# Moving the first transposes of a batch behind the GEMM before them, on one core of a fused attention and feed-forward kernel

## The chip, the cores and the metric

The kernel runs on one core of a Trainium2 chip. The metric is the device time of one execution in microseconds (us); the kernel before takes 343.51 us (median of 3 runs, 342.83 to 344.71). A profiled execution gives a trace; its span (first to last instruction) is some 2 us shorter than the device time (339.1 of 341.0 us before the change, 343.0 of 345.15 after it). Each run also has a mean granted clock of TensorE (PE), as a share of full speed. PE does matmuls and transposes, ACT (ScalarE) the exponentials and GELUs, DVE (VectorE) copies and normalisation, POOL (GpSimd) the weighing of v, the causal masks and the issue of some loads; SP issues the other transfers.

## The reference

Batch 8, 8 heads, 576 tokens, head size 64; then a feed-forward block 512 to 2048 to 512 on all 4608 tokens.

```python
scores = (1 / sqrt(D)) * q @ k.T
cum    = cumsum(log(clip(f, 0.0001, 1.0)), axis=-1)
scores = where(causal, -1e9, scores + cum[..., :, None] - cum[..., None, :])
attn   = softmax(scores)                         # max subtracted, sum + 1e-9
x      = (attn @ v).transpose(0, 2, 1, 3).reshape(B * S, H * D)
out    = gelu_exact(x @ w_in) @ w_out
```

In the softmax the row's own `cum` cancels; what is left is a weight per key. The kernel multiplies v by it once ("weighing") and takes the weight itself as one more column of v, which gives the denominators.

## The kernel before

Work goes by batches, and within a batch by pairs of heads (0 to 3), each with four score tiles (0 to 3). POOL kept to the order in which the program lists its lines, and a line that waited held up what stood behind it: in the trace of the changed kernel it stood idle for 3.79 us ahead of the third weighing, and the first masks of pair 2, listed behind it, started at 54.09, though the exponentials of that pair had ended by 51.85. v has one buffer, in two halves: heads 0 to 3 (pairs 0 and 1) and heads 4 to 7 (pairs 2 and 3).

```python
def load_v(b, h0=0, h1=H):                 # five transfers, issued by SP
    for n in range(NBLK):
        p0 = D if n == NBLK - 1 else 0
        nc.sync.dma_start(v_sb[p0:P, h0:h1, n, :], v[b, h0:h1, ...])   # cut

def weigh_v(b, i, eng=nc.gpsimd):          # one pair's v, on POOL
    eng.tensor_tensor(vw(b)[:, hs, :, 0:D], v_sb[:, hs, :, :], w..., Alu.mult)   # L268
    if b: eng.tensor_copy(vw(b)[:, hs, :, D], w)

def behind(t, h):                          # makes POOL wait until t has landed
    nc.gpsimd.tensor_copy(g[:PT], t[:, h, 0:1])

# scores(b, i, t): matmuls (L299), exponential on ACT (L309), then, but for the
# first pair, the causal mask on POOL:
nc.gpsimd.affine_select(out=et[:, :, c0 + z : c0 + P], ...)             # L311
```

Batch 1's attention, with parts of batch 0's second GEMM as fill (`take(fill, n)`, L517). `transposes(i, ...)` puts a pair's q and k through PE (L207) and copies them out on DVE (L216); `run(i)` is a pair's attention (L330), and `to_xT` transposes what came of a pair for the first GEMM (L363).

```python
tiles(0, 0)
transposes(1, o_psum, "o")
transposes(2, m_psum, "m")
tiles(0, 2)
transposes(3, m_psum, "m")
tiles(1, 0)
run(0)
tiles(1, 2)
take(fill, 4)
weigh_v(1, 2)
tiles(2, 0)
run(1)
weigh_v(1, 3)
# ... cut: tiles 2 and 3 of pairs 2 and 3, in part shown in the diff
run(2)
```

And in the first GEMM of batch 0 (16 blocks `ffb`, each followed by its GELU):

```python
if ffb == 14:
    for which in range(2):
        transposes_first(1, 0, which, o_psum, "o")
if ffb == 12:
    behind(qk_of[1][0], H - 1)
    nc.gpsimd.memset(v_sb[:, 4:8, 0, 0:1], 0.0)   # releases the next load
    load_v(1, 4, 8)
    weigh_v(1, 0)
    load_w_out(1)
    weigh_v(1, 1)
    load_qk_tokens(2)
```

The softmax here doesn't subtract the row's maximum and nothing guards it: scores larger than these inputs give would overflow.

Of the kernel before, what the change touches and what calls it, by code (L numbers as in the profile page):

```python
# [17 lines left out]
H = 8  # L18
# [34 lines left out]
def kernel(  # L53
# [10 lines left out]
    nc = tc.nc  # L64
# [24 lines left out]
    o_psum = ctx.enter_context(tc.tile_pool(name="o_psum", bufs=2, space=PSUM))  # L89
    m_psum = ctx.enter_context(tc.tile_pool(name="m_psum", bufs=2, space=PSUM))  # L90


    qk_of = {}
# [79 lines left out]
    def load_w_out(c):  # L173
        kt = slice(c * n_ff // 4, (c + 1) * n_ff // 4)
        nc.gpsimd.dma_start(w_out_sb[:, kt, :], w_out_r[:, kt, :])
# [25 lines left out]
    def transposes_first(b, i, which, pool, tag):  # L201

        src = qk_of[b][which]
        ps = pool.tile([P, JT, PT], BF16, tag=tag, name="ps_f")
        for j in range(JT):
            for h in range(2):
                nc.tensor.transpose(  # L207
                    ps[h * D : (h + 1) * D, j, :],
                    src[:, 2 * i + h, j * D : (j + 1) * D],
                    ident_bf[:PT, :PT],  # L210
                )

        dst = (qT, kT)[which][i].rearrange("d (p j) -> d p j", j=JT)
        src = ps.rearrange("d j p -> d p j")
        if b or i:
            nc.vector.tensor_copy(dst, src)  # L216
        elif which:
            nc.vector.tensor_copy(dst[:, 0 : PT // 2], src[:, 0 : PT // 2])
            nc.scalar.copy(dst[:, PT // 2 :], src[:, PT // 2 :])
        else:  # L220
            nc.scalar.copy(dst, src)
# [36 lines left out]
    def vw(b):  # L258
        if b not in vw_of:
            vw_of[b] = v_pool.tile([P, H, NBLK, D + 1], BF16, tag="vw", name=f"vw{b}")  # L260
        return vw_of[b]

    def weigh_v(b, i, eng=nc.gpsimd):

        hs = slice(2 * i, 2 * i + 2)
        bh = b * H + 2 * i
        w = wT[:, :, bh : bh + 2].rearrange("p n h -> p h n")
        eng.tensor_tensor(  # L268
            vw(b)[:, hs, :, 0:D],
            v_sb[:, hs, :, :],  # L270
            w.unsqueeze(3).to_broadcast([P, 2, NBLK, D]),
            Alu.mult,
        )
        if b:
            eng.tensor_copy(vw(b)[:, hs, :, D], w)
# [47 lines left out]
    def attend(b, i, h, ms):  # L323
        if (b, i, h) not in o_of:
            o_of[b, i, h] = o_psum.tile([P, NBLK, D + 1], FP32, tag="o", name="o")
        o = o_of[b, i, h]
        for m in ms:
            for n in range(m + 1):
                t, c = where(n, m)
                nc.tensor.matmul(  # L330
                    o[:, m, :],
                    e_of[b, i, t][:, h, c : c + P],
                    vw_of[b][:, 2 * i + h, n, :],
                    start=(n == 0),
                    stop=(n == m),
                )
# [14 lines left out]
    def xT(b):  # L351
        if b not in xT_of:
            xT_of[b] = xT_pool.tile([P, n_dm, XC], BF16, tag="xT", name="xT")
        return xT_of[b]

    def to_xT(b, i, copy, pool=m_psum, tag="m", ps=None):
        if ps is None:
            shape = [P, 2, 1024] if pool is s_psum else [P, XC]
            ps = pool.tile(shape, BF16, tag=tag, name="ps_x")
            if pool is s_psum:  # L360
                ps = ps[:, 0, 0:XC]
        for m in range(NBLK):
            nc.tensor.transpose(  # L363
                ps[:, m * P : (m + 1) * P], x_of[b, i][:, m, :, :], ident_bf
            )
        copy(xT(b)[:, i, :], ps)
# [7 lines left out]
    def x_tail(b):  # L374
        nc.gpsimd.tensor_copy(tails[:, :, b * TL : (b + 1) * TL], xT(b)[:, :, XC - TL :])
# [125 lines left out]
    def gemm2_half(c, half):  # L501

        pss = [
            m_psum.tile([P, d_model], FP32, tag="m", name="ps2") for _ in range(2)
        ]
        k0, k1 = half * n_ff // 2, (half + 1) * n_ff // 2
        if half:
            order = [(ts, kt) for ts in range(2) for kt in range(k0, k1)]
        else:
            order = [  # L510
                (ts, kq + kt)
                for kq in (0, 4)
                for ts in range(2)
                for kt in range(4)
            ]
        for ts, kt in order:
            nc.tensor.matmul(  # L517
                pss[ts],
                g_of[c][kt][:, ts * P : (ts + 1) * P],
                w_out_sb[:, kt, :],  # L520
                start=(kt == k0),
                stop=(kt == k1 - 1),
            )
            if kt == k1 - 1 and not half:
                ot_of.append(o_pool.tile([P, d_model], FP32, tag="ot", name="ot"))
                (nc.scalar.copy if ts else nc.vector.tensor_copy)(ot_of[ts], pss[ts])
            elif kt == k1 - 1:
                nc.vector.tensor_tensor(ot_of[ts], ot_of[ts], pss[ts], Alu.add)
                store(c, ts, ot_of[ts])
            yield  # L530
# [6 lines left out]
    def take(gen, n):  # L537
        for _ in range(n):
            if next(gen, "end") == "end":
                return  # L540
# [7 lines left out]
    def behind(t, h):  # L548

        g = x_pool.tile([P, 1], FP32, tag="gate", name="gate")  # L550
        nc.gpsimd.tensor_copy(g[:PT], t[:, h, 0:1])
# [140 lines left out]
    def second_attention():  # L692


        b, fill = 1, gemm2_half(0, 0)

        def av(i, h):
            attend(b, i, h, (0, 1, 2, 3, 4))
            normalize(b, i, h)

        def transposes(i, pool, tag):
            for which in range(2):
                transposes_first(b, i, which, pool, tag)


        nc.scalar.activation(warm[0:1, 0:1], warm[0:1, 0:1], Act.Exp)
        def tiles(i, t):
            scores(b, i, t)
            scores(b, i, t + 1)

        def run(i):
            av(i, 0)
            av(i, 1)

        tiles(0, 0)
        transposes(1, o_psum, "o")
        transposes(2, m_psum, "m")
        tiles(0, 2)
        transposes(3, m_psum, "m")
        tiles(1, 0)  # L720
        run(0)
        tiles(1, 2)
# [5 lines that stand above are left out]
        tiles(2, 2)  # L728
        take(fill, 4)
        tiles(3, 0)  # L730
        transpose_dma(2, 0, 4)
        transpose_dma(2, 4, 8)
        take(fill, 4)
        to_xT(b, 0, nc.vector.tensor_copy, o_psum, "o")
        tiles(3, 2)
        behind(qk_of[2][1], H - 1)
        load_w_out(2)
        load_w_out(3)
        run(2)
        to_xT(b, 1, nc.vector.tensor_copy, o_psum, "o")  # L740
        take(fill, 4)
        av(3, 0)
        both = s_psum.tile([P, 2, 1024], BF16, tag="s", name="ps_x2")
        to_xT(b, 2, nc.scalar.copy, ps=both[:, 0, 0:XC])
        av(3, 1)
        gemm1_begin(1, both)
        x_tail(1)
        load_v(2)

    for b in range(B):  # L750
        if b == 0:
            first_attention()
        elif b == 1:
            second_attention()
        else:
            attention(b)
        if b == 0:
            x_tail(0)
        for ffb in range(4 if b < 2 else 5, n_ff):
            gemm1(b, ffb, ps=spare() if b > 1 and ffb in (7, 8) else None)  # L760
            if b == 0:
                if ffb == 14:
                    for which in range(2):
                        transposes_first(1, 0, which, o_psum, "o")
                if ffb == 12:
                    behind(qk_of[1][0], H - 1)
                    nc.gpsimd.memset(v_sb[:, 4:8, 0, 0:1], 0.0)
                    load_v(1, 4, 8)
                    weigh_v(1, 0)
                    load_w_out(1)  # L770
                    weigh_v(1, 1)
                    load_qk_tokens(2)
            elif b + 1 < B:
                first, gap = (5, 3) if b == 1 else (1, 4)
                at, late = divmod(ffb - first, gap)
                if late == 0:
                    untangle(b + 1, at)
                if late == gap - 2 and (b > 1 or at < 2):
                    weigh_v(b + 1, at)
                if ffb == (9 if b == 1 else 14):  # L780
                    load_qk_tokens(b + 2)
# [34 lines left out]
```

## Time and profile before

| | before |
|---|---|
| device time, median of 3 | 343.51 us |
| span and granted clock of the profiled run | 339.1 us, 0.998 |
| first exponential of batch 1 | 40.31 us |
| last piece of v, heads 4 to 7, landed | 47.13 us |
| POOL's third weighing (pair 2) | 47.37 us |
| PE: attention of pair 2, of pair 3 | 52.30, 54.91 us |
| first GELU of batch 0, of batch 1 | 25.59, 58.69 us |

The profiled execution took 341.0 us and is not one of the three timed ones. The first exponential and the tail of the attention are what the change goes for. The weighing of pair 2 is what turned out to matter: it starts 0.24 us after its v has landed. The distance from the first GELU of batch 0 to that of batch 1 (33.10 us here) is the cleanest measure of the stretch that is changed, as it leaves out how the kernel's start went in a run; I use it below. Lines of the profile stand in the prediction.

### The profile page before, as it was taken

Reading aid. Unit: us, or ns where it says so; the run is one execution under the profiler, and the core shown is the slowest. Engines: PE = TensorE matmul, PEld = TensorE weight load, DVE = VectorE, ACT = ScalarE, POOL = GpSimd, SP = SyncE. Lnnn points to the kernel's source line nnn. Section 1 sums busy time; section 2 is a strip of 40 time slices with the busy share of each in tenths; the row PEclk is TensorE's granted clock in tenths of the full one; section 3 lists DMA queues with packets and bytes.
Section 4 is the critical chain, followed back from the end, with each engine's and each line's share of the span. In section 5 each row is a group of like instructions: output and inputs, shape, how many; then the busy total and the mean of one; then the engine's idle time right before and its main releaser. Section 6 shows DMA issues by size and latency. Waiting matters only on the chain.

```text
span 339.1 us, 7794 instructions
## 1 busy us (share of the span) xinstructions
PE 325.5 (96%) x3129; PEld 171.6 (51%) x3170; DVE 184.3 (54%) x417; ACT 209.9 (62%) x299; POOL 121.5 (36%) x250
## 2 busy tenths in 40 slices
PE   8799899999999999999999999999999999999995
PEld 4574455445554456445644565446544654444443
DVE  4770446664358935895579646974696541020011
ACT  6977786773735787378737873787368755404600
POOL 8190395037437053713453343624351420000000
PEclk9999999999999999999999999999999999999999
DMA  7999999979999799299959598589900241011013
GB/s 118 180 167 192 210 186 143 194 143 188 209 172 181 116 205 189 83 139 130 223 132 138 112 198 177 77 137 208 173 31 2 82 80 44 0 63 64 0 38 88
DMA packets 104628, 44.18 MB, mean 130 GB/s; under 512 B 83408, under 2 KB 100048, under 8 KB 104592
## 3 DMA queue, kind: packets, MB, share of 16 engines
q1 hardware_dynamic: 87296, 29.52, 45.4%
q0 software_dynamic: 16896, 13.63, 27.1%
q8 instruction: 25, 0.41, 0.5%
q10 hardware_dynamic: 400, 0.52, 0.4%
q14 instruction: 11, 0.09, 0.1%
HBM read 36.85 MB, written 9.44 MB: 137 GB/s over the span
## 4 chain that ended last, share of the span: by engine, by line
PE 90%; issue 2%; DMA 2%; ACT 2%; POOL 1%; DVE 1%; SPq 0%; POOLq 0%; DVEq 0%; ACTq 0%
PE ps L385 36%; PE ps L479 26%; PE o L330 10%; PE ps L421 8%; PE s L299 7%; DMA v_sb<-in_v_dram 2%; PE ps L517 2%; ACT e L309 1%; PE ps_x L363 1%; POOL q L107 1%; SPq L119 0%; POOL k L107 0%; PE ps_f L207 0%; DVE x L344 0%; DVE vw L268 0%
## 5 line engine op out<-in xcount | busy, mean ns | idle before, releaser
L405 ACT ACTIVATE g<-ps 128x512 bf16<-128x512 f32 x144 | 82.1, 601 | 80.3 <-PE ps L385 80.3
L309 ACT ACTIVATE e<-s 128x896 bf16<-128x896 f32 (+2 forms) x128 | 100.8, 834 | 26.6 <-PE s L299 24.5
L385 PE MATMUL ps<-xT,w_in_sb 128*128 128x512 bf16 x502 | 111.8, 379 | 0.5
L479 PE MATMUL ps<-w_out_sb,g 64*128 64x512 bf16 (+1 forms) x712 | 101.9, 376 | 0.8 <-issue 0.5
L385 PEld LDWEIGHTS <-w_in_sb 128*128 128x128 bf16 x576 | 55.9, 98 | 67.6 <-issue 1.8
L311 POOL TENSOR_SCALAR_AFFINE_SELECT e<-e 128x256 bf16<-128x256 bf16 (+1 forms) x135 | 49.1, 383 | 93.6 <-ACT e L309 93.3
L479 PEld LDWEIGHTS <-g 64*128 64x128 bf16 (+1 forms) x736 | 41.9, 94 | 39.8 <-issue 9.0
L299 PE MATMUL s<-qT,kT 64*128 64x320 bf16 (+4 forms) x384 | 45.6, 276 | 3.5 <-ACT e L309 2.3
L268 POOL TENSOR_TENSOR vw<-v_sb,wT 128x640 bf16<-128x640 f32 x30 | 38.6, 1289 | 24.9 <-PE s L299 14.5
L249 DVE COPY qT<-tq 64x288 bf16<-64x288 bf16 x96 | 42.2, 440 | 3.4 <-DMA tq<-q 2.0
L249 DVE COPY kT<-tk 64x288 bf16<-64x288 bf16 x96 | 40.7, 424 | 2.4 <-DMA tk<-k 0.8
L487 DVE COPY ot<-ps 128x512 f32<-128x512 f32 x25 | 17.3, 692 | 41.8 <-PE ps L479 41.8
L330 PE MATMUL o<-vw,e 128*128 128x65 bf16 x960 | 36.6, 194 | 3.0 <-issue 2.4
L330 PEld LDWEIGHTS <-e 128*128 128x128 bf16 x960 | 34.1, 98 | 6.8 <-POOL e L311 2.5
L344 DVE TENSOR_TENSOR x<-o,r 128x320 bf16<-128x320 f32 x64 | 31.5, 492 | 2.4 <-DMA xT<-x 0.2
L430 DVE COPY ot<-ps 128x512 f32<-128x512 f32 (+2 forms) x9 | 5.7, 632 | 48.9 <-PE ps L421 46.1
L299 PEld LDWEIGHTS <-kT 64*128 64x128 bf16 x384 | 19.7, 94 | 24.3 <-issue 11.7
L421 PE MATMUL ps<-w_out_sb,g 128*128 128x512 bf16 (+2 forms) x142 | 27.9, 355 | 0.1
L343 DVE RECIPROCAL r<-o 128x5 f32<-128x5 f32 x64 | 12.1, 190 | 22.9 <-PE o L330 22.7
L421 PEld LDWEIGHTS <-g 128*128 128x128 bf16 x144 | 13.5, 98 | 14.5
L490 DVE TENSOR_TENSOR ot<-ot,ps 128x512 f32<-128x512 f32 x25 | 17.2, 687 | 1.4
L385 PE MATMUL ps<-tails,w_in_sb 128*128 128x512 bf16 x62 | 14.2, 377 | 0.2
(67 smaller groups left out, 133.6 us busy)
## 6 DMA issues: line engine op xcount, KB each, us to landing
out_dram<-ot SPq DMA_DIRECT2D x32, 256.0 KB, 2.6
v_sb<-in_v_dram SPq DMA_DIRECT2D x24, 256.0 KB, 4.8
q<-in_q_dram POOLq DMA_DIRECT2D x6, 576.0 KB, 6.3
k<-in_k_dram POOLq DMA_DIRECT2D x6, 576.0 KB, 8.3
v_sb<-in_v_dram SPq DMA_DIRECT2D x22, 128.0 KB, 4.9
w_in_sb<-in_moe_w_in_dram POOLq DMA_DIRECT2D x4, 512.0 KB, 7.9
w_out_sb<-in_moe_w_out_dram POOLq DMA_DIRECT2D x4, 512.0 KB, 9.0
q<-in_q_dram POOLq DMA_DIRECT2D x4, 144.0 KB, 4.4
```

Source lines behind the costliest of these rows:

```text
L249: nc.vector.tensor_copy(rows[:, odd], src[odd * D : (odd + 1) * D, 2 * i + h].rearrange("d j p -> d p j"),)
L268: eng.tensor_tensor(vw(b)[:, hs, :, 0:D], v_sb[:, hs, :, :], w.unsqueeze(3).to_broadcast([P, 2, NBLK, D]), Alu.mult,)
L299: nc.tensor.matmul(to, *ab, start=half < 0, stop=half == 1 or not masked)
L309: nc.scalar.activation(et[:, :, z:c], st[:, :, z:c], Act.Exp, scale=scale)
L311: nc.gpsimd.affine_select(out=et[:, :, c0 + z : c0 + P], in_=et[:, :, c0 + z : c0 + P], compare_op=Alu.is_ge, fill=0.0, base=z, pattern=[[ ...
L330: nc.tensor.matmul(o[:, m, :], e_of[b, i, t][:, h, c : c + P], vw_of[b][:, 2 * i + h, n, :], start=(n == 0), stop=(n == m),)
L344: nc.vector.tensor_tensor(x_of[b, i][:, :, h, :], o[:, :, 0:D], r.unsqueeze(2).to_broadcast([P, NBLK, D]), Alu.mult,)
L385: nc.tensor.matmul(ps, w_in_sb[:, kt, ffb * P : (ffb + 1) * P], src[:, kt, 0:TC], start=(kt == 0), stop=(kt == n_dm - 1),)
L405: nc.scalar.activation(g_of[c][ffb], ps, Act.Gelu)
L421: nc.tensor.matmul(pss[ts][:, c0:c1], g_of[c][kt][:, ts * P : (ts + 1) * P], w_out_sb[:, kt, c0:c1], start=(kt == 0), stop=(kt == n_ff - 1),)
L479: nc.tensor.matmul(banks[r], g_of[c][kt][rows, ts * P : (ts + 1) * P], w_out_sb[rows, kt, :], start=kt == (steps.index("r") if r else 0), ...
L487: nc.vector.tensor_copy(ot, banks[1])
```

## The change

The intent: the first pair's transposes no longer stand ahead of the GEMM's last block; all others go into the wait for the first exponential; less work is left behind the last. With the early transposes goes the gate that guarded them, and with it the order of the lines behind that gate.

```diff
+        transposes(0, o_psum, "o")
         tiles(0, 0)
         transposes(1, o_psum, "o")
         transposes(2, m_psum, "m")
+        transposes(3, o_psum, "o")
         tiles(0, 2)
-        transposes(3, m_psum, "m")
+        take(fill, 2)
         tiles(1, 0)
@@ tail of batch 1's attention
-        take(fill, 4)
         to_xT(b, 0, nc.vector.tensor_copy, o_psum, "o")
+        to_xT(b, 1, nc.vector.tensor_copy, o_psum, "o")
+        take(fill, 2)
         tiles(3, 2)
@@ (cut)
         run(2)
-        to_xT(b, 1, nc.vector.tensor_copy, o_psum, "o")
         take(fill, 4)
@@ first GEMM of batch 0
-                if ffb == 14:
-                    for which in range(2):
-                        transposes_first(1, 0, which, o_psum, "o")
                 if ffb == 12:
-                    behind(qk_of[1][0], H - 1)
+                    weigh_v(1, 0)
                     nc.gpsimd.memset(v_sb[:, 4:8, 0, 0:1], 0.0)
                     load_v(1, 4, 8)
-                    weigh_v(1, 0)
                     load_w_out(1)
```

## The prediction

> **What bounds the kernel now.** I read the page first, then the chain of waits, then the timelines of PE, ACT, DVE and POOL over batch 1's attention (36 to 59 us), then the DMA view of single stretches.
>
> ```profile
> PE 325.5 (96%) x3129; PEld 171.6 (51%) x3170; DVE 184.3 (54%) x417; ACT 209.9 (62%) x299; POOL 121.5 (36%) x250
> ...
> PE 90%; issue 2%; DMA 2%; ACT 2%; POOL 1%; DVE 1%; SPq 0%; POOLq 0%; DVEq 0%; ACTq 0%
> ```
>
> PE carries 90% of the chain; only where ACT, POOL or a DMA holds it up is there anything to win or lose. The change touches one such place. PE there:
>
> ```profile
> 36.59 0.45 PE L207 MATMUL ps_f<-key_of,q 96*64 96x96 bf16 x12
> 36.87 0.42 PE L207 MATMUL ps_f<-key_of,k 96*64 96x96 bf16 x12
> 37.22 1.04 PE L385 MATMUL ps<-xT,w_in_sb 128*128 128x512 bf16 x4
> ...
> 41.25 0.36 PE L299 MATMUL s<-qT,kT 64*128 64x448 bf16 x2 [0.83 <-ACT e L309]
> ...
> 53.76 0.45 PE L363 MATMUL ps_x<-key_of,x 128*128 128x128 bf16 x5 [0.34 <-DVE x L344]
> ```
>
> The transposes of pair 0 stand ahead of the GEMM's last block, so the last GELU, the table load and the exponentials come later; PE then waits 0.83 us for the first exponential, and 0.34 us behind the last scores. These are the waits that the change aims at. ACT runs exponentials from 40.31 to 53.63 us, with gaps of about 1 us in all. POOL shows a dependence that the intent does not mention:
>
> ```profile
> 37.55 0.18 POOL L551 CAST gate<-q 96x1 f32<-96x1 bf16 x1 [12.01 <-DMA q<-in_q_dram]
> 37.67 0.10 POOL L767 MEMSET v_sb<- 128x4 f32 x1
> 39.70 1.27 POOL L268 TENSOR_TENSOR vw<-v_sb,wT 128x640 bf16<-128x640 f32 x1 [1.93 <-PE ps_f L207]
> ...
> 47.37 1.28 POOL L268 TENSOR_TENSOR vw<-v_sb,wT 128x640 bf16<-128x640 f32 x1 [0.22 <-POOL e L311]
> ```
>
> The memset at 37.67 releases the load of v for heads 4 to 7 (the first of its five transfers is issued at 37.79). The weighing at 39.70 needs v of heads 0 to 3, whose last piece was issued at 26.13 and took 13.4 us: 39.5. So it waited for that DMA, not for the PE instruction named. The weighing at 47.37 needs v of heads 4 to 7; its last piece was issued at 39.87 and took 7.3 us: landed 47.1. It too starts when v lands, with no slack. How fast v moves depends on its company. Three stretches, 30 to 36, 41 to 43 and 43 to 54 us (packets, MB, share):
>
> ```profile
> q0 software_dynamic: 1148, 0.86, 91.1%
> q1 hardware_dynamic: 1149, 0.29, 36.2%
> ```
> ```profile
> q1 hardware_dynamic: 1670, 0.41, 95.7%
> q0 software_dynamic: 41, 0.03, 11.0%
> ```
> ```profile
> q0 software_dynamic: 2090, 1.70, 101.3%
> q1 hardware_dynamic: 971, 0.24, 17.9%
> ```
>
> Beside the loads of POOL's queue (q0), v (q1, 256-byte packets) gets packet for packet: 191 per us each. Alone it gets 835 per us. It now goes through in 41 to 43 us, in the hole between two loads of q0.
>
> [...] masks follow the weighing on POOL. [...] the first warm-up matmuls are 427 ns apart until about 6.5 us, against 216 ns later, and the granted clock falls 2.3 us after the last matmul. [...] the load at 38.91 took 1.28.
>
> **The change part by part.**
>
> *Pair 0 behind the GEMM's last block.* 24 transposes take 0.63 us (36.59 to 37.22). Block 15 starts at 36.59 instead, its GELU at about 37.67 instead of 38.30, and the table is there at 39.7 instead of 40.3. The copies of q and k (started 0.49 us behind the transposes) now run from 37.94 to 39.36, the scores start at 39.42 and the first tile is ready at about 40.0. So the first exponential comes at 40.0, not 40.31: a gain of 0.3 us.
>
> *Pair 3 moved ahead of tiles 2 and 3.* It takes the two PSUM buffers of pair 1, and must wait for DVE to copy pair 1 out. A copy each 0.67 us: pair 1's run from 40.56 to 41.98, so pair 3's k transposes can only start at 42.03 and tile 2's scores at 42.30, against 41.25 before. The third exponential slips from 41.80 to about 42.85: a loss of 1.05 us, which ACT carries along at 0.8 to 1.0.
>
> *Less behind the last.* Before the last tiles, four matmuls become two plus five more transposes: 0.15 us won. Behind them one transpose group and its wait go (0.34 + 0.29). With the exponentials ending 0.8 us later, the last pair's attention starts 0.2 us later than before (55.1 against 54.91). These parts sum to nearly nothing.
>
> *The gate.* The gate on q goes and the first weighing moves ahead of the memset. So v of heads 4 to 7 is no longer released at 37.77 but when v of heads 0 to 3 has landed and been weighed: 39.70 + 1.27 + 0.2 for the cast + 0.1 = 41.2, 3.4 us later. The next load of W_out and the loads of q and k for batch 2 go out as before (41.1, 43.3, 44.1). v misses the hole: its packets start some 2.5 us after the issue (the packets before show this), at 43.7, and W_out's at 43.3. From there q0 has 512 + 768 + 768 packets: 512 at 155 per us (425 to 430 in 2.8 us, before, with W_in's 1 KB packets) is 3.3 us, 1536 at 191 is 8.0 us, so q0 is busy to 54.6. v's 2304 packets get 430 + 1540 in that time and the last 330 in 0.4 us alone; with 0.3 us to land, v is there at 55.3, not 47.1.
>
> The weighing of pair 2 then starts at 55.55. Before, the masks of pair 2's tiles ended 4.5 us after it (47.37 to 51.85, with the other weighing between). So PE can start pair 2's attention at 60.05, not 52.3. Then 1.05 us of attention and 0.87 us of fill, and pair 3's attention starts at 62.0, against 54.91: +7.1 us. The masks of pair 3 end at about 61.7, just in time. From here on all is in order as before.
>
> *The clock.* PE would stand idle from 53.3 to 60.1 us, 6.8 us. [...] The sum: 7.1 + 2.2 = 9.3, less 0.3 for batch 2's transfers having more time, so about +9.0 us on 343.5: 352.5.
>
> **The rivals.**
> 1. *v still lands in time.* If v's share of the DMA engines is better than packet for packet, or the weighing at 39.70 comes earlier, POOL is no limit as long as v lands by 48.5. For it: v moved at four times the rate in 41 to 43. Against it: that hole is over before v is issued, and in 30 to 36 it got no more than 1:1. Then only the PE and ACT parts count: 343 to 344, the same.
> 2. *The intent works.* If pair 3's transposes did not wait for pair 1's copies, the exponentials would start 0.3 us earlier and the tail lose 0.6 us: 342.7. Against it: eight copies of 0.67 us on DVE, of which four can be done before tile 2, and the same two buffers. Still the same by 2%.
> 3. *v lands late, but PE's clock holds*[...]: 350.5, at the 2% line (350.4).
> 4. *v even slower*, as the first half was: 15.3 us from its first packet (24.2) to its landing. Then v lands at 59 and the time is near 356.
>
> **Range and chances.** I give rival 1 and 2 together 14%, rival 3 or a landing some 2 us sooner another 12%. Range 346 to 355. Faster by over 2%: 0.01; within 2%: 0.25; slower: 0.74.
>
> **What would show it.** The first exponential at about 40.0 and the third near 42.85. POOL's third weighing with a wait of several us on the DMA of v, starting at about 55.5. A PE gap of 5 to 8 us ahead of pair 2's attention, released by POOL. A granted clock below 1 in the us behind it, and fill matmuls 427 ns apart. Batches 2 to 7 unchanged in length. I am wrong if v lands before 49 us: then the time stays within 1 us.

## The result, and the profile after

| | before | after |
|---|---|---|
| device time, median (range), 6 runs each on one chip | 343.17 (342.60 to 344.71) | 347.15 (345.15 to 349.61) |
| ratio of the fast runs, 95% interval | | 1.0111 (1.0066 to 1.0157) |
| span and granted clock of the profiled run | 339.1, 0.998 | 343.0, 0.999 |
| first exponential of batch 1 | 40.31 | 40.67 |
| third exponential | 41.80 | 43.58 |
| last piece of v, heads 4 to 7, landed | 47.13 | 52.20 |
| third weighing | 47.37 | 52.71 |
| attention of pair 2, of pair 3 | 52.30, 54.91 | 56.89, 58.92 |
| first GELU of batch 0, of batch 1 | 25.59, 58.69 | 26.20, 62.70 |

Ratios here and below are the mean time of one kernel's fast runs over that of the other's of the same rounds, so not quite the ratio of the medians beside them. By the line at 2% the two are the same; but the interval does not hold 1, and every one of these six runs of the changed kernel took longer than each of the six of the one before. It is slower by 1.1%, some 3.8 us, where the prediction had 9.0. Of the 4.0 us at the first GELU of batch 1, 0.6 was there at the first GELU of batch 0, which the change does not touch. The stretch between them grew from 33.10 to 36.50 us: +3.4. The batches behind it kept their length (first GELU of batch 1 to that of batch 7: 223.8 us in both).

The page of the changed kernel, the two lines that answer to those of before:

```profile
PE 329.3 (96%) x3170; PEld 171.4 (50%) x3170; DVE 184.5 (54%) x417; ACT 210.3 (61%) x299; POOL 121.6 (35%) x249
...
PE 83%; DMA 7%; SPq 4%; POOL 4%; issue 1%; DVE 0%; POOLq 0%
```

PE's share of the busy time is unchanged (its count is higher only because before's trace lacks some matmul records), so the first line shows nothing. The chain of what ended last does: DMA went from 2% to 7%, and POOL and SP's queue have 4% each. (These shares are not the loss: the chain now also runs back through the 13.61 us flight of v's first half, beside which PE was busy with the GEMM.) Followed in order of time (start, duration, what), the chain passes through the stretch like this:

```profile
44.26 7.94 DMA v_sb<-in_v_dram
...
54.16 0.93 POOL e L311 x3
55.09 1.25 POOL vw L268
...
57.25 0.97 PE o L330 x25
```

Read it downwards: v's last piece is in flight for 7.94 us, then POOL's masks and weighings, then PE's attention of pair 2. On POOL (start, busy time, engine, line, operation, and in brackets the idle time ahead and what ended it):

```profile
40.21 1.28 POOL L268 TENSOR_TENSOR vw<-v_sb,wT 128x640 bf16<-128x640 f32 x1 [14.06 <-DMA v_sb<-in_v_dram]
41.58 0.10 POOL L766 MEMSET v_sb<- 128x4 f32 x1
...
52.71 1.28 POOL L268 TENSOR_TENSOR vw<-v_sb,wT 128x640 bf16<-128x640 f32 x1 [3.79 <-DMA v_sb<-in_v_dram]
```

The memset that releases the load of heads 4 to 7 now stands behind the first weighing, at 41.58 instead of 37.67 (3.3 us later, counted from the first GELU of batch 0), and the first weighing waits for heads 0 to 3. The third weighing has a wait of 3.79 us for the load; before it had 0.22 and another releaser. And PE:

```profile
38.06 0.45 PE L207 MATMUL ps_f<-key_of,q 96*64 96x96 bf16 x12
...
40.03 0.28 PE L299 MATMUL s<-qT,kT 64*128 64x256 bf16 x2 [1.26 <-DVE kT L216]
...
54.55 0.23 PE L330 MATMUL o<-vw,e 128*128 128x65 bf16 x2 [0.53 <-POOL e L311]
56.89 1.33 PE L330 MATMUL o<-vw,e 128*128 128x65 bf16 x28 [2.11 <-POOL e L311]
```

The transposes of pair 0 have moved from 36.59 to 38.06, behind the GEMM; the price is a wait of 1.26 us for DVE's copy of k, which used to lie beside the last block. The new gaps are the last two: PE stands before pair 2's attention and waits for POOL's masks, which wait for v. On ACT, the first and third exponentials of the stretch:

```profile
40.67 1.62 ACT L309 ACTIVATE e<-s 128x896 bf16<-128x896 f32 x2 [0.39 <-PE s L299]
43.58 3.05 ACT L309 ACTIVATE e<-s 128x896 bf16<-128x896 f32 x4 [1.29 <-PE s L299]
```

Counted from the first GELU of batch 0, the first exponential came 0.25 us sooner (14.47 against 14.72). The third then had to wait 1.29 us for scores which stood behind pair 3's transposes.

Where did v's packets go? q0 is POOL's queue (W_out, then q and k of batch 2), q1 is SP's (v). Three stretches of the changed kernel, 44 to 46, 47 to 48 and 49 to 51 us (packets, MB, share of the 16 DMA engines):

```profile
q0 software_dynamic: 299, 0.31, 105.0%
```
```profile
q1 hardware_dynamic: 998, 0.25, 111.8%
q0 software_dynamic: 23, 0.01, 10.4%
```
```profile
q0 software_dynamic: 409, 0.31, 100.2%
q1 hardware_dynamic: 281, 0.07, 26.9%
```

In the first stretch W_out moves and v not at all, although v's second transfer was issued at 42.1. In the second v has the engines nearly to itself. In the third v shares with q and k, and gets two packets for three of theirs.

### The profile page after: what moved, and what is told of

It reads as the page before. It is cut to its first block, busy times and chain, and to the rows that moved or that the text cites. A ratio compares the mean times of both kernels' runs of the same rounds, so it can differ in the third digit from the quotient of the medians.

```text
span 343.0 us, 7834 instructions
## 1 busy us (share of the span) xinstructions
PE 329.3 (96%) x3170; PEld 171.4 (50%) x3170; DVE 184.5 (54%) x417; ACT 210.3 (61%) x299; POOL 121.6 (35%) x249
## 4 chain that ended last, share of the span: by engine, by line
PE 83%; DMA 7%; SPq 4%; POOL 4%; issue 1%; DVE 0%; POOLq 0%
PE ps L385 32%; PE ps L479 27%; PE ps L421 8%; PE o L330 8%; DMA v_sb<-in_v_dram 7%; PE s L299 6%; SPq L119 4%; POOL vw L268 1%; PE ps L517 1%; POOL q L107 1%; POOL e L311 0%; POOL k L107 0%; DVE vw L268 0%; POOL w_in_sb L171 0%; PE ps_x L363 0%
## 5 line engine op out<-in xcount | busy, mean ns | idle before, releaser
L479 PE MATMUL ps<-w_out_sb,g 64*128 64x512 bf16 (+1 forms) x736 | 108.5, 377 | 0.0
L249 DVE COPY kT<-tk 64x288 bf16<-64x288 bf16 x96 | 41.6, 433 | 2.5 <-DMA tk<-k 0.9
L249 DVE COPY qT<-tq 64x288 bf16<-64x288 bf16 x96 | 41.5, 433 | 1.4
L216 DVE COPY qT<-ps_f 128x576 bf16<-128x576 bf16 x7 | 5.3, 754 | 17.0 <-PE ps_f L207 17.0
```

What stands on the lines that cost most here:

```text
L249: nc.vector.tensor_copy(rows[:, odd], src[odd * D : (odd + 1) * D, 2 * i + h].rearrange("d j p -> d p j"),)
L479: nc.tensor.matmul(banks[r], g_of[c][kt][rows, ts * P : (ts + 1) * P], w_out_sb[rows, kt, :], start=kt == (steps.index("r") if r else 0), ...
```

## The experiments

All ran correct, 6 runs each (e6 has 5), each beside 11 runs of the kernel before on the same chip. Every run counted as fast but one of e2 (350.76 us, which is left out of its ratio). By the line at 2%, e5, e8 and e9 are unclear and all others the same as before. "GELU to GELU" is the distance from the first GELU of batch 0 to that of batch 1 in the profiled run; "half clock" is how long the granted clock was half there within 55 to 66 us; "v landed" is the last piece of heads 4 to 7. Times in us.

| run | what | ratio to before | median | v landed | half clock | GELU to GELU |
|---|---|---|---|---|---|---|
| (before) | | 1 | 343.17 | 47.13 | 0 | 33.10 |
| (after) | | 1.0111 | 347.15 | 52.20 | 0 | 36.50 |
| e1 | after, old gate block | 0.9988 | 341.78 | 46.97 | 0 | 33.35 |
| e2 | before, new gate block | 1.0152 | 347.94 | 50.71 | 3.41 | 37.00 |
| e3 | e1, pair 3 moved back | 0.9984 | 341.78 | 46.97 | 0 | 33.58 |
| e4 | after, PE kept busy | 1.0134 | 347.04 | 51.78 | 0 | 36.81 |
| e5 | after, W_out issued first | 1.0236 | 350.45 | 55.61 | 10.24 | 42.71 |
| e6 | after, q and k later | 1.0104 | 345.64 | 49.98 | 0 | 35.96 |
| e7 | after, v released with no gate | 1.0005 | 342.05 | 44.74 | 0 | 33.34 |
| e8 | after, again | 1.0155 | 348.02 | 54.10 | 6.83 | 41.35 |
| e9 | after, W_out behind second weighing | 1.0166 | 346.83 | 50.10 | 3.41 | 36.82 |
| e10 | before, shorter tail alone | 0.9975 | 340.50 | 45.00 | 0 | 32.48 |
| e11 | e5, PE kept busy | 1.0169 | 347.16 | 51.38 | 0 | 38.95 |

**My theory:** the whole loss comes from the release of v, which waits for the other half of v; the moved transposes and the shorter tail together sum to nearly nothing. **The rival:** the loss is PE's and ACT's own, from the transposes that left the shadow of block 15 and from the third exponential's wait.

### The gate undone, and the gate alone (e1, e2)

e1 is the changed kernel with the old block:

```diff
-                    weigh_v(1, 0)
+                    behind(qk_of[1][0], H - 1)
                     nc.gpsimd.memset(v_sb[:, 4:8, 0, 0:1], 0.0)
                     load_v(1, 4, 8)
+                    weigh_v(1, 0)
```

> The whole change, but with the gate on q back and the load of v for heads 4 to 7 released ahead of the first weighing, as before. My theory: the loss is all in v's late release, and the moved transposes sum to nearly nothing, so 343.4 us (342.8 to 344.2, before 343.2); POOL's third weighing (pair 2) starts at 47.5 to 48.5 us without a wait of several us on v, no PE gap over 0.6 us ahead of pair 2's attention; the third exponential still comes about 1 us later than in the kernel before. Rival (the transposes' new order is what costs): stays at 346 to 347.

e2 is the kernel before with only this edit reversed: the new order of these lines, nothing else of the change.

> The kernel before with only the gate's change: the first weighing ahead of the memset, and no gate on q. My theory: the whole loss is here, 347 us (345.5 to 349), v of heads 4 to 7 lands at 51 to 55 us, POOL's third weighing waits 3 us or more for it, PE stands idle for 2 to 6 us ahead of pair 2's attention, and in most runs the granted clock falls to 0.990 to 0.996. Rival (the transposes cost): 343 to 343.5, the same as before.

e1 took 341.78 us, ratio 0.9988 (0.9950 to 1.0026). v landed at 46.97, and the third weighing no longer waits for it:

```profile
48.54 1.28 POOL L268 TENSOR_TENSOR vw<-v_sb,wT 128x640 bf16<-128x640 f32 x1 [0.22 <-POOL e L311]
```

e2 took 347.94, ratio 1.0152 (1.0106 to 1.0199). Its third weighing waited 3.84 us for v, and PE has the same gap as in the changed kernel:

```profile
55.40 1.91 PE L330 MATMUL o<-vw,e 128*128 128x65 bf16 x28 [2.11 <-POOL e L311]
```

The rival falls: with every moved transpose in place but the release as before, no loss is seen; with the release alone, all of it is.

### v released without any gate (e7)

```diff
-                    weigh_v(1, 0)
                     nc.gpsimd.memset(v_sb[:, 4:8, 0, 0:1], 0.0)
                     load_v(1, 4, 8)
+                    weigh_v(1, 0)
```

> The changed kernel with v of heads 4 to 7 released at once, by a memset with nothing ahead of it (about 25 us): neither the gate on q nor the weighing. v's second half then follows its first half on the same queue and should be through by 44 us, with q and k of batch 1 as late as before (39.5 us) since v's queue had one packet in two anyway. So the time of the run with the gate undone: 0.995 to 1.003. Rival (the gate protected q and k): k's second half lands at 41 us or later, pair 2's transposes wait, 1.003 or more.

342.05 us, ratio 1.0005 (0.9973 to 1.0037), and the third weighing again waits for masks (0.21 us) and not for v. The old gate on q, which the change was right to take for unneeded, can go; what counts is that the memset does not stand behind the first weighing.

### Pair 3 back where it was (e3)

From e1, pair 3's transposes return behind tiles 2 and 3 of pair 0, to ask what the third exponential's wait is worth:

```diff
-        transposes(3, o_psum, "o")
         tiles(0, 2)
-        take(fill, 2)
+        transposes(3, m_psum, "m")
@@ behind pair 1's tiles
-        take(fill, 4)
+        take(fill, 6)
```

> As the run with the gate undone, and besides pair 3's transposes back behind tiles 2 and 3 in the other PSUM pool, with the two fill matmuls back behind pair 1's tiles; so only pair 0's move and the shorter tail are left of the change. My theory: pair 3's transposes wait for DVE's copies of pair 1 and hold up the third exponential by 1 us; without that the third exponential follows the second at once, and the time is 0.5 to 1.0 us below the run with the gate undone and below before: 342.5 us. Rival (ACT and PE have slack there): equal to the run with the gate undone within 0.2 us.

341.78 us, the same as e1, ratio 0.9984 (0.9956 to 1.0013). The wait did not go, it moved. The third exponential now follows at once, but the fifth waits:

```profile
44.33 3.03 ACT L309 ACTIVATE e<-s 128x896 bf16<-128x896 f32 x4 [0.94 <-PE s L299]
```

In both versions PE's transposes of pair 3 wait for DVE's copies out of the buffers that they are to fill (0.57 and 0.22 us in e3). So moving pair 3 alone wins nothing: both versions have pair 0 behind the GEMM, and in both the copies set the pace. The loss of 1.05 us that the prediction had ACT carry along is there in e1's trace: counted from the first GELU of batch 0, its exponentials end at 29.05 us, and those of before at 28.04. Why it does not show in e1's time is seen in e10.

### The same kernel again (e8)

> The changed kernel itself again, for a second trace and more runs beside the others on one chip: 1.009 to 1.014 of before. v of heads 4 to 7 lands at 50 to 53 us; PE's gap ahead of pair 2's attention is 2 to 3.5 us, and the clock either falls in it (then the fill matmuls behind it are 427 ns apart and the span is 1 to 2 us longer) or not.

348.02 us (344.22 to 349.07), ratio 1.0155 (1.0106 to 1.0205), over what was expected. The profiled run is the slowest of the six. In this trace v landed at 54.10, later than the expected 50 to 53, and PE's gaps were 3.14 and 2.12 us. v's first transfer had been issued at 40.37, against 41.71 in the first trace of the change: sooner by 1.34 us and landed later by 1.90, so the time of the release does not set the landing by itself. The granted clock was half for 6.83 us from 57.30 on. By stretches of 4 us, with the busy time of PE, weight loads, DVE, ACT and POOL, then PEclk, DMA share and GB/s; first the profiled run of the change, then e8:

```profile
58.00:62.00 4.00, 4.00 (x58) 2.56 (x55) 2.77 (x8) 2.56 (x3) 2.52 (x6) 1.00 0.94 136
```
```profile
58.00:62.00 4.00, 3.18 (x32) 2.13 (x33) 1.37 (x4) 0.00 (x0) 4.00 (x12) 0.50 1.00 183
```

At a clock of 0.50 PE finished 32 matmuls in this stretch, not 58, the rest of its gap included. From the start of pair 2's attention to the first GELU of batch 1 it took 8.04 us, against 5.81 in the profiled run of the change, and the GELU-to-GELU distance was 41.35: +8.25 on before, close to the predicted +9. So a stretch as long as the predicted one does occur, in some executions. How much of it is the clock, the six runs do not say: two of them had a mean clock of 0.99 too and yet spans of 342.3 and 342.7 us, less than the 343.0 of the change's profiled run at 0.999.

### W_out ahead of the first weighing (e5)

To have W_out out of v's way, its load goes out first:

```diff
                 if ffb == 12:
+                    load_w_out(1)
                     weigh_v(1, 0)
                     nc.gpsimd.memset(v_sb[:, 4:8, 0, 0:1], 0.0)
                     load_v(1, 4, 8)
-                    load_w_out(1)
```

> The changed kernel with one line moved: the load of W_out's second quarter is issued ahead of the first weighing, so it follows the first quarter at once (41 to 44 us) and is not in v's way. v is still released late (41 to 42 us). My theory that v is late because of its company: v of heads 4 to 7 lands at 46 to 48.5 us, POOL's third weighing starts without a wait of several us, and the time is that of the run with the gate undone, 0.995 to 1.003 of before. Rival (the late release alone makes it late, whoever else loads): v lands at 50.5 or later, and 1.009 to 1.013 of before.

350.45 us, ratio 1.0236 (1.0194 to 1.0278): the theory that v only needs W_out out of its way falls, and the rival's 1.009 to 1.013 was missed as well. In the trace the first two transfers landed by 46.95, in the hole behind W_out; the other three met q and k of batch 2 and landed at 50.38, 53.79 and 55.61. From 48 to 53 us:

```profile
q0 software_dynamic: 939, 0.71, 90.4%
q1 hardware_dynamic: 928, 0.23, 35.6%
```
```profile
56.13 1.28 POOL L268 TENSOR_TENSOR vw<-v_sb,wT 128x640 bf16<-128x640 f32 x1 [7.79 <-DMA v_sb<-in_v_dram]
```
```profile
60.31 1.92 PE L330 MATMUL o<-vw,e 128*128 128x65 bf16 x28 [2.06 <-POOL e L311]
```

Here v moved packet for packet beside q0 to about 1% (928 to 939), as the prediction had it, and its numbers come out: landing 55.61 (predicted 55.3), weighing 56.13 (55.55), attention 60.31 (60.05). That is in part luck: the order of the loads is another than the one that was predicted, and a second trace of this order (e11) has the landing at 51.38. The clock was half for 10.24 us.

### PE kept busy through the gap (e4, e11)

Matmuls whose result nobody reads, ahead of pair 2's attention, take the idle time away, not the wait: 16 in the changed kernel (e4), 26 in e5's (e11).

```diff
+        keep = o_psum.tile([P, TC], FP32, tag="o", name="ps_w")
+        for _ in range(16):     # 26 in e11
+            nc.tensor.matmul(keep, key_of[:, 0:P], w_in_sb[:, 0, 0:TC], start=True, stop=True)
         run(2)
```

> The changed kernel with 16 matmuls of 512 columns (3.5 us) into an unused PSUM tile ahead of pair 2's attention, where PE stands idle for v. They use an idle engine. My theory that part of the loss is PE's clock falling in the gap: granted clock 0.997 or more in all runs, where the changed kernel had 0.990 to 0.994 in five of six, and 345.5 us, some 1.5 us below the changed kernel's 347.15. Rival (the clock's fall costs nothing, since the matmuls behind it wait anyway): 347 us as before.

> The kernel of the run with W_out's load first, in which v landed latest (55.6 us), PE stood idle from 53.4 to 60.3 us but for two small matmuls, and the clock was at half for 10.2 us; now with 26 matmuls of 512 columns (5.6 us) on PE in that gap, over by 59 us, before POOL's masks are ready. If the clock's fall has a price of its own, some 2 us as predicted: granted clock 0.997 or more in all runs instead of 0.984 to 0.990, no stretch at half clock behind the gap in the trace, fill matmuls 216 ns apart, and about 1.017 of before instead of 1.0236. If the fall costs nothing: 1.022 to 1.025, whatever the clock.

e4 missed its 345.5 and is inconclusive on the median: 347.04 us, ratio 1.0134 (1.0096 to 1.0172), no gain over the change. Its 16 matmuls ran to 57.10, some 0.3 us past the masks, and do not cover a gap that lasts longer in another run. What it shows lies in its own six runs: three at a clock of 0.999 or more have spans of 343.5 to 344.6 us, three at 0.99 or less 345.8 to 346.9, on average 2.4 us more. Landing and clock may differ together there, so this is an upper bound.

e11 took 347.16, ratio 1.0169 (1.0140 to 1.0199) against e5's 1.0236: 0.0067 of 342 us is 2.3 us won, as expected; how the landings of the two sets of runs differ is not known, so this difference alone does not show the cause. All its runs had a clock of 0.995 or more; e5's had 0.984 to 0.990. In its trace the idle matmuls themselves set the start of the attention:

```profile
53.35 5.79 PE L744 MATMUL ps_w<-w_in_sb,key_of 128*128 128x512 bf16 x25
```

The attention followed at 58.97, and from there to the first GELU of batch 1 it took 5.59 us, where e5 took 8.01 at half clock. That difference, 2.4 us, is within one stretch of PE work and does not depend on when v came. With e8 against the change (8.04 and 5.81, 2.2 us) it sizes 6.83 us (e8) and 10.24 us (e5) at half clock. With 3.41 us at half clock, in e9, the same stretch took 7.33 us, 1.5 us over 5.81. (v landed at 51.38 in e11's trace and at 55.61 in e5's with the same order of loads: the two traces differ by 4 us in the landing.)

### q and k of batch 2 later, W_out later (e6, e9)

Two ways to clear v's path by what competes with it. e6 issues q and k of batch 2 behind the third weighing; e9 issues W_out behind the second.

```diff
# e6                                        # e9
         weigh_v(1, 2)                                load_v(1, 4, 8)
+        load_qk_tokens(2)                  -         load_w_out(1)
@@ first GEMM of batch 0                              weigh_v(1, 1)
-                    load_qk_tokens(2)      +         load_w_out(1)
```

> The changed kernel with the loads of q and k for batch 2 issued only behind POOL's third weighing. If q and k beside v cost what the prediction said (packet for packet to the end), v now lands at 48.5 to 49.5 us instead of 52; if W_out alone held v back, the first four of v's five transfers land as in the changed kernel (44.3, 48.6, 49.3, 50.5) and only the fifth is earlier. The issue of the two loads takes POOL 1.6 us ahead of pair 2's masks, so pair 2's attention can start some 6.1 us behind the third weighing, at about 55.5 us: 1.004 to 1.008 of before, against 1.011 for the changed kernel.

> The changed kernel with the load of W_out's second quarter issued behind the second weighing instead of ahead of it, 1.5 us later (43 us); v is still released only by the first weighing. If v stands still because W_out's and then q's and k's packets are in its way, and not because it is released late, its first four transfers now go alone between 42.5 and 45 us at 800 to 900 packets per us, v has landed by 48.5 us, POOL's third weighing does not wait over 1 us, and the time is 0.996 to 1.004 of before. If the late release alone decides, v lands at 50 or later and the time is 1.009 or more.

e6: 345.64 us, ratio 1.0104 (1.0067 to 1.0142), outside the expected 1.004 to 1.008. W_out landed at 48.27, and v's last four transfers between 48.99 and 49.98, 0.5 us past the expected range. The second and third came no sooner than in the changed kernel (48.99 and 49.48 against 48.64 and 49.26), so in this trace it was not q and k that held these up; the fourth and fifth gained 0.7 and 2.2 us. But q and k of batch 2 now came at 57.4 and 60.3, and the profiled run pays at 107 and 109 us:

```profile
108.90 3.40 PE L385 MATMUL ps<-xT,w_in_sb 128*128 128x512 bf16 x15 [1.07 <-DMA xT<-x]
```

That wait, and one of 0.69 us just before, are new: from the first GELU of batch 1 to that of batch 7 it took 226.4 us instead of 223.8. The gain comes back as a larger loss.

e9: 346.83 us, ratio 1.0166 (1.0129 to 1.0204); missed. Three of v's transfers landed by 44.69, but from 45 to 47 us W_out moved 317 packets and v 49, and the fourth and fifth landed at 47.69 and 50.10. v had been first by 1.3 us in the order of issue, and that did not help its later pieces. PE's gap was 1.51 us, and behind it the clock was half from 55.11 to 58.52 in the profiled run (the 28 matmuls of the attention took 1.91 us there, 1.33 in the change's); its mean was 0.995 or less in all six.

### The tail alone (e10)

Before, with only the moved `to_xT` and the fill behind it:

```diff
-        take(fill, 4)
         to_xT(b, 0, nc.vector.tensor_copy, o_psum, "o")
+        to_xT(b, 1, nc.vector.tensor_copy, o_psum, "o")
+        take(fill, 4)
         tiles(3, 2)
@@ (cut)
         run(2)
-        to_xT(b, 1, nc.vector.tensor_copy, o_psum, "o")
```

> The kernel before with only pair 1's transposes for x moved ahead of the last two tiles, in front of the same four fill matmuls. By the prediction's working the last scores come 0.3 us later and the tail loses 0.6 us, so pair 3's attention starts some 0.35 us earlier: 0.997 to 1.000 of before. Rival (ACT's chain sets the end, the tail had slack): 1.000 to 1.001.

340.50 us against 341.17 for before on this chip, ratio 0.9975 (0.9944 to 1.0006). GELU to GELU it is 0.6 us shorter (32.48 against 33.10), which is the figure that the prediction's second rival gives for the tail. It is the fastest version tried, but the interval holds 1: a gain of 0.6 us fits the runs and is not proven by them.

Beside e1 it shows what "nearly nothing" was made of. GELU to GELU, e1 has 33.35 us: 0.87 more than e10, though it has the same shorter tail. In the traces of e1, e3, e7 and the change, all with pair 0 behind the GEMM, DVE's first copy of pair 1 starts 14.97 or 14.98 us behind the first GELU of batch 0; in those of before and e10 it starts at 14.11, also 0.87 sooner. So pair 0's move brought the first exponential 0.25 us forward and DVE's copies 0.87 us back, and the tail's gain hid the cost. No run has pair 0's move alone, and the ratios (0.9988 and 0.9975) do not separate e1 from e10, so this rests on single traces.

## Why the prediction was right or wrong

**Right: where the loss comes from.** The release of v moves behind the first weighing, v misses its hole, POOL waits, and PE waits for POOL. e1 and e2 show that this one edit is the whole loss, and the traces have each step in its order.

**Right: the other parts sum to nearly nothing.** e1, with all of them, has a ratio of 0.9988. The gain at the first exponential was 0.25 us (0.3 predicted). The third exponential waited as predicted, 2.09 us behind the second instead of 0.69; e3 shows that moving pair 3 back only moves the wait. In e1 pair 3's attention starts 0.25 us later than before, counted from the first GELU of batch 0 (0.2 predicted). The zero is a sum of a gain of some 0.6 us in the tail and a loss of some 0.9 ahead of it (e10).

**Right: what follows from the landing.** From the third weighing to pair 2's attention it took 4.18 us (4.5 predicted), from there to pair 3's 2.03 (1.95 predicted).

**Wrong: the landing.** The step that failed is "v's 2304 packets get 430 + 1540 in that time and the last 330 in 0.4 us alone; with 0.3 us to land, v is there at 55.3". In the profiled run of the change v landed at 52.20. What was wrong in it is the way of v beside q0's three loads, taken to follow on each other with no break. The 430 packets predicted beside W_out were not a sharing: v moved 528 packets from 42 to 44 us, before W_out's got going, and then none from 44 to 46 while W_out moved 299. After that came a hole that the term did not have, between W_out's packets and those of q and k: v moved 998 packets from 47 to 48 us beside 23 of q0, where the measured 191 per us beside q0 would have given it 191. Some 640 of the 2304 were left; of these, 425 moved from 48 to 49 us beside 147 of q0, and only the rest shared with q and k, one for one at most, as the term had it. At one for one with q0, 191 packets per us, the 807 more packets of that one microsecond are worth 4.2 us, an estimate from these counts, which is more than the 3.1 us between 52.20 and 55.3. In e5, whose hole took only the first two transfers, the landing was 55.61, close to the predicted 55.3. The trace of the kernel before held a warning: from 44 to 46 us, beside W_out and q, v's last transfer, whose issue was over by 42.40, got 92 packets to q0's 389, and not packet for packet.

**Wrong: taking the landing for one number.** The change landed at 52.20 in one trace and 54.10 in another (e8), and the order of e5 at 55.61 and 51.38 (e11). With the two others that release v late (e2, 50.71; e4, 51.78), the predicted 55.3 lies at the late end of what occurs, and the runs of the change spread over 4.5 us where those of before spread over 2.1.

**Half right: the clock.** What the trace of before had shown was a start at 427 ns per matmul and a clock that fell 2.3 us behind the last one; that it would fall in the gap, and the 2.2 us for it, were estimates of mine. The size stands: 2.2 (e8) and 2.4 (e5 against e11) were measured from pair 2's attention to the next GELU. But it was taken as paid in every run. The profiled run of the change, its fastest, did not pay it; its other five have clocks of 0.994 and 0.990. A stretch of 3.41 us at half clock, as in e2 and e9, lowers the mean by 3.41 x 0.5 / 343 = 0.005, so I estimate some 3.4 us at half clock in three of them and some 6.8 us, as in e8, in the others. Their median is 347.58, 2.4 us above the profiled run; how late v landed in them is not known, so not all of it need be the clock. And the single idle stretch of 6.8 us was 0.53 and 2.11 us in the profiled run.

**The sum.** Of the predicted 9.0 us, the profiled run has 3.4: the landing came 3.7 us sooner than predicted, counted from the first GELU of batch 0 (26.0 against 29.7), and the estimated 2.2 us of clock were not paid; smaller terms make up the rest. The mean over runs, some 3.8 us, includes part of the clock. The predicted mechanism with a late landing and a fall of the clock is e5's and e8's trace (10.24 and 6.83 us at half clock). A chance of 0.74 for more than 2% was too sure: it rested on one landing and one clock, and the rival that it gave 12%, a sooner landing or a clock that holds, is what the profiled run showed, with both; in the five others the clock fell, and their landings were not traced.

**What stays open.** Why v's transfers stood still beside W_out in the change (0 packets to 299) and nearly so in e9 (49 to 317), though they shared one for one with W_in's equally large packets before (425 to 430) and with q and k in e5 and e8 (939 to 928 and 561 to 552). The experiments shift what v meets; none shows whether v's packets were ready in the queue and not served, or not ready. And which executions fall to half clock is not settled: gaps of 0.44 and 2.11 us (e2) and of 1.51 us (e9) were followed by 3.41 us of it, gaps of 0.53 and 2.11 us (the profiled run of the change) by none.

## What to carry to other kernels

When an edit removes a gate or swaps two lines on an engine, follow every load that these lines release before counting what the edit was meant for; here a memset behind one weighing, 3.9 us later, cost all that was lost. Check, too, whether a sum of nearly nothing hides a gain worth keeping: the tail alone was the fastest version tried. Take the landing time of a load from a spread of runs, not from one rate: here a hole of one microsecond in q0 let 998 packets of v through, worth an estimated 4.2 us. Price an idle PE twice, once as the gap and once as a slower clock behind it (1.5 us in e9, 2.2 in e8, 2.4 in e5, none in the profiled run of the change), and give the second a probability of its own.
